# Lent buffers, other PSUM banks and a new step order in a fused chunked-attention and top-1 MoE kernel

## The chip, the cores and the metric

The kernel runs on 1 core of one Trainium2 chip, as one launch. The metric is the device time in microseconds (us) of one execution. Three runs of the kernel before stand beside the one execution that the profiler recorded. PE is TensorE, DVE is VectorE, ACT is ScalarE, POOL is GpSimd, and SP is the engine whose queue issues nearly all loads and stores.

## The reference

Attention inside chunks of 64 rows, then a mixture of 8 experts in which each token takes one expert. A token whose local gate is 0.5 or more takes over the expert of the token before it.

```
q, k, v: (8, 8, 576, 64)                      # batch, heads, rows, head size; fp32
per chunk of 64 rows: attn = softmax(q k^T / 8); x = attn v
x: (8, 576, 512)                              # heads side by side
logits = x w_gate (512 x 8); gate = sigmoid(x w_local)
e[s] = argmax(logits[s])  if s == 0 or gate[s] < 0.5  else  e[s-1]
out[s] = softmax(logits[s])[e[s]] * (relu(x[s] w1[e]) w2[e])     # w1: 512 x 1024, w2: 1024 x 512
```

## The kernel before, in words

**Attention.** The 4608 rows are 18 blocks of 256 rows. Each block loads q, k and v (512 KB each), pairs the heads anew (`pair_heads`, POOL copies into `qr`, `kr`), transposes them on PE (`trans4`, L195, into `qT`, `kT`), forms scores (L230) and the softmax (`pr`), transposes P (L195, into `pT`), multiplies with v (`values`, L279, into `xs`), transposes x (`xT`), forms the router's logits (`router`: L321, a copy to `lT`, the transposes L330, a reduction), and stores x with its logits to `x_d` in DRAM (528 KB, L343). One block in each nine, at place `LEFT`, holds the 64-row remainders of four batches and is loaded in other pieces (L146). v lies in pieces of 64 floats (256 B) in DRAM.

The order of steps is written by hand in `PAR`: "start", then "steady" once per i = 1 to 15 (L869), then "drain". A word such as `tp*8` takes the next eight parts of the step `tp`. In iteration i the words mean: `lq` loads q and k of block i+5 and `lv` loads v of block i+2 (SP); `s` scores of i+1; `va` values of i-1; `tx` transposes of x(i-2); `tq` transposes of q and k of i+2; `ra` the router of i-2 (its first part L321, its second L330 and the store); `tp` transposes of P(i); `pr` POOL's copies of i+3; `h0` to `h3` are places at which routing steps run ("hooks": 4 times the iteration, plus the place). Every engine and SP's queue work in exactly this order. q and k have three buffer pairs, so the load of block i+5 waits for POOL's copies of block i+2; v has three buffers (one of them lies in `raw2`), so the load of v(i+2) waits for the values of block i-1.

**Drain and routing.** The last blocks run through "drain" together with the routing: `ex` is a list of DVE operations whose last results are `regs` (L953, L929), words that every engine reads into registers to decide branches (`word` L983, `test` L990), and `ehot` (L950).

**Experts.** Tokens come by expert in tiles of 128, gathered from `x_d`. Each product has three passes with weights split into a high and a low part. `two(a)` works on two tiles: `up_pair` (L1040, matmuls L1046) if both have the same expert, else `up` for each, then `next_x`, which transposes the x of the next tiles (L688), `h_atoms`, which transposes the hidden layer `hsb` (L688), and `down` (L743), whose scaled output `ysb` (L1074) is scattered to `out` (L804). PSUM has eight banks: `TR[0..2]`, two of `HB`, two `YB`, one `MB`. After the pairs, `rest(t)` takes tile after tile, with a `VALID` test that leaves when no tile is left.

Of the kernel before, what the change touches and what calls it, by code (L numbers as in the profile page):

```python
# [8 lines left out]
F32 = mybir.dt.float32  # L9
# [29 lines left out]
LEFT = 4  # L39
# [12 lines left out]
        "p0*4 t0a*4 t0a t0b*4 t0b t0c*4 t0c t0d*4 t0d p1*4 q3 t1a*4 t1a s0*8 t1b*4 t1b s0*2 t1c*4 t1c "  # L52
        "q4 t1d*4 t1d p2*4 s0*4 s1*8 t2a*4 t2a t2b*4 t2b s1*2 o0*4 o0 o0*4 o0 s1 t2c*4 t2c t2d*4 t2d s1*3 q5 v2 p3*4 io "
# [18 lines left out]
    "steady": "lq va*4 va s*8 s h0 tx*8 tq*8 s h1 va*4 lv ra*2 va h2 tq*8 ra*2 tp*8 s pr*4 h3 ",  # L72
    "hooks": [43, 43, 45, 46, 47, 48, 49, 49, 51, 51, 52, 53, 54, 55, 55, 56, 57, 58, 59, 61, 61, 62],
# [4 lines left out]
def tile_attention_then_moe(ctx: ExitStack, tc, q, k, v, wg, wl, w1, w2, out):  # L78
# [17 lines left out]
    w2h = [wpool.tile([P, 2, C], F32R, name=f"w2h{c}") for c in range(4)]  # L96
    w2l = [wpool.tile([P, 2, C], F32R, name=f"w2l{c}") for c in range(4)]
# [27 lines left out]
    vbuf = [[raw2[c].rearrange("p f (h d) -> p (f h) d", d=2 * D) for c in (2, 3)]]  # L125
# [29 lines left out]

    def load_v(i):
        vt = vbuf[i % 3]
        t0 = 0
        for b, s0, n in place(i)[1]:
            for s1 in range(s0, s0 + n, P):  # L160
                m = min(P, s0 + n - s1)
                nc.sync.dma_start(
                    vt[t0 // P][t0 % P:t0 % P + m, :, 0:D],
                    v[b, :, s1:s1 + m, :].rearrange("h s d -> s h d"),
                )
                t0 += m
        return vt
# [191 lines left out]
    cnt = cpool.tile([P, E], F32, name="cnt")  # L359
# [187 lines left out]
    const = {}  # L547

    def constants():
        pcol = iota([P, 1], [[0, 1]], cm=1, name="pcol")  # L550
        pcol1 = iota([P, 1], [[0, 1]], base=1, cm=1, name="pcol1")
        iota_r = iota([P, P], [[1, P]], dst=pa2.tile([P, P], BF16, name="iota_r", tag="xT", bufs=1))
# [29 lines left out]
        const.update(pcol=pcol, pcol1=pcol1, iota_m=iota_m, iota_h=iota_h, iota_hp=iota_hp, iota_t=iota_t, iota_e=iota_e, idxm8=idxm8, padidx=padidx, upper=upper, ones=ones, zrow=zrow, notfirst=notfirst, hot0=hot0)  # L582
# [10 lines left out]
    nc.sync.dma_start(wg9[:, :, 0:8], wg.rearrange("(c p) e -> p c e", p=P))  # L593
    nc.sync.dma_start(wg9[:, :, 8:9], wl.rearrange("(c p) e -> p c e", p=P))
    with tc.manual_schedule(engines=MAN | {ET.Pool}):
        warm = cpool.tile([P, 1], F32, name="warm")
# [15 lines left out]
        st |= dict(  # L612
            io=lambda: [constants], s0=lambda: a_sa(0, True), q3=load(qk, load_qk, 3),
            s1=lambda: a_sa(1, True), o0=lambda: a_tp(0, True), q4=load(qk, load_qk, 4), q5=load(qk, load_qk, 5),
            v2=load(vts, load_v, 2))
        for i in range(3):
            for g in range(4):
                st[f"t{i}{'abcd'[g]}"] = lambda i=i, g=g: tq(i, g)
        play(PAR["start"], st)
    pcol, pcol1, iota_m, iota_h, iota_hp, iota_t, iota_e, idxm8, padidx, upper, ones, zrow, notfirst, hot0 = (  # L620
        const[n] for n in "pcol pcol1 iota_m iota_h iota_hp iota_t iota_e idxm8 padidx upper ones zrow notfirst hot0".split())
# [247 lines left out]
    for i in range(1, NS - 2):  # L869
# [58 lines left out]
    def plus(o, a, k, b):  # L928
# [21 lines left out]
        lambda: V.tensor_tensor(ehot, te[:, 0:NTILE].unsqueeze(2).to_broadcast([P, NTILE, E]),  # L950
                                iota_e.unsqueeze(1).to_broadcast([P, NTILE, E]), ALU.is_equal),
# [7 lines left out]
        plus(regs[:, 0], flags[:, 3, 0:NTILE], VALID, sums[:, 0]),  # L959
    ]  # L960
# [79 lines left out]
    def up_pair(a, f0):  # L1040
        hbs = [(f, TR[f // 2 % 3]) for f in (f0, f0 + 2)]
# [57 lines left out]
    def two(a):  # L1099
# [17 lines left out]
        def next_x():  # L1117
            atoms = [x_atoms(a + 2 + n, ps) for n, ps in enumerate((TR[1], MB)[:1 + (a + 2 in PAIRS)])]
            for f in atoms:
                run(f[:2])  # L1120
            late_x[:] = [f[2] for f in atoms]

        def second():
            run(pr[:2])
            with tc.If(test(a, SAME, WORK)) as cmp:
                up_pair(a, 4)
                next_x()
            with cmp.Else():
                for g in range(2):
                    run(h_atoms(a, g, TR[1 - g]))  # L1130
                rejoin_h(a)
                up(a + 1)
                next_x()
                for g in range(2):
                    run(h_atoms(a + 1, g, TR[2 - 2 * g]))
# [8 lines left out]
        rejoin_h(a + 1)  # L1144

    def body(t):
# [20 lines left out]
        down(t - 1, (3,), (1,))  # L1167

    def rest(t):
        if t == NTILE:  # L1170
            down(t - 1)
            return
        if t < TMIN:
            body(t)
            rest(t + 1)
            return
        with tc.If(test(t, VALID, ALL, want=0)) as cmp:  # L1177
            nc.gpsimd.drain()
            down(t - 1)
        with cmp.Else():  # L1180
            body(t)
            rest(t + 1)
# [5 lines left out]
    with tc.manual_schedule(engines=MAN | {ET.SP, ET.Pool}):  # L1188
# [29 lines left out]
        rest(PAIRS[-1] + 2)  # L1218
# [21 lines left out]
```

## Time and profile before

| | |
|---|---|
| median of three runs | 644.95 us (644.72 to 646.14) |
| the profiled execution | 645.8 us |
| its span in the trace | 643.8 us, mean granted clock 0.996 |
| PE busy | 608.2 us, 94% of the span |
| DVE, ACT, POOL busy | 380.1 (59%), 256.4 (40%), 146.8 us (23%) |
| DMA packets | 78355, of them 42672 under 512 B |

The span is the time between the first and the last instruction in the trace; the other 2.0 us of the profiled execution lie around it. In a list of instructions "[0.80 <-ACT hsb L789]" says that the engine stood idle for 0.80 us before the row and that the operation of line 789 on ACT, which writes `hsb`, ended the wait. In the table of windows, "16.80 (x401)" is busy time and the number of instructions.

### The profile page before, as it was taken

How to read it: one execution, taken by the hardware profiler on the slowest of the kernel's cores; microseconds unless marked ns; L12 is line 12 of the kernel's file. 1: busy time of each engine (PE TensorE's matmuls, PEld its weight loads, DVE VectorE, ACT ScalarE, POOL GpSimd, SP SyncE). 2: the span in 40 equal slices, each digit the busy share in tenths (PEclk: the TensorE clock that was granted, in tenths of full speed). 3: DMA queues.
4: the chain of work that ended last, by engine and by line, in shares of the span. 5: the costliest groups of instructions: out<-in, count | busy, mean ns of one | idle time of the engine just before them, and what ended most of it. 6: DMA issues, size and time to landing. Idle time of an engine off the chain costs nothing. (4 is left out here: it accounts for less than half of the span.)

```text
span 643.8 us, 17179 instructions
## 1 busy us (share of the span) xinstructions
PE 608.2 (94%) x5904; PEld 513.8 (80%) x5904; DVE 380.1 (59%) x990; ACT 256.4 (40%) x468; POOL 146.8 (23%) x217
## 2 busy tenths in 40 slices
PE   4898898999999999999999999999999999999995
PEld 4787776776778878689899997789988998688883
DVE  2676676996785757476433565773478533387231
ACT  4676685774411152532212433431365211343120
POOL 3632253570060302022021021022011221011201
PEclk9999998999999999999999999999999999999999
DMA  8899999989531155055121164441176511054100
GB/s 261 231 261 291 255 273 303 311 244 305 167 125 43 53 167 181 20 182 179 37 69 52 28 217 152 150 175 49 43 240 225 192 52 59 29 184 145 67 26 35
DMA packets 78355, 97.83 MB, mean 152 GB/s; under 512 B 42672, under 2 KB 46768, under 8 KB 78192
## 3 DMA queue, kind: packets, MB, share of 16 engines
q1 hardware_dynamic: 71744, 75.30, 37.7%
q0 software_dynamic: 6160, 19.99, 9.3%
q8 instruction: 84, 1.38, 0.9%
q14 instruction: 79, 0.65, 0.3%
q10 hardware_dynamic: 288, 0.52, 0.3%
HBM read 76.62 MB, written 19.69 MB: 150 GB/s over the span
## 5 line engine op out<-in xcount | busy, mean ns | idle before, releaser
L804 POOL DMA_INDIRECT out<-ysb,sidx x38 | 40.2, 1058 | 359.6 <-DVEq L1024 160.9
L743 PE MATMUL y<-w2h,hq 128*128 128x512 f32 x368 | 119.8, 395 | 1.8 <-DVE ysb L1074 1.8
L1046 PE MATMUL tr<-xp,w1h 128*128 128x256 f32 x704 | 90.1, 283 | 1.5 <-ACTq L1024 1.5
L1046 PEld LDWEIGHTS tr<-xp,w1h 128*128 128x128 f32 x704 | 87.8, 192 | 4.4 <-ACTq L1024 1.9
L743 PEld LDWEIGHTS y<-w2h,hq 128*128 128x128 f32 x368 | 69.1, 188 | 17.2 <-issue 3.0
L743 PE MATMUL y<-w2l,hq 128*128 128x512 f32 x184 | 71.8, 390 | 0.0
L1054 ACT ACTIVATE hq<-tr 128x256 fp32r<-128x256 f32 x68 | 25.3, 384 | 110.0 <-PE tr L1046 76.5
L743 PE MATMUL y<-w2h,hp 128*128 128x512 f32 x192 | 63.3, 397 | 0.3 <-ACT hp L690 0.3
L722 PE MATMUL h<-w1h,xp 128*128 128x512 f32 x208 | 60.5, 396 | 0.0
L1055 DVE SCALAR_TENSOR_TENSOR hq<-tr,hq 128x256 fp32r<-128x256 f32 x68 | 28.2, 423 | 41.3 <-ACT hq L1054 38.9
L1046 PE MATMUL tr<-xp,w1l 128*128 128x256 f32 x352 | 47.6, 283 | 0.0
L1074 DVE TENSOR_SCALAR ysb<-y,ppr 128x512 f32<-128x512 f32 x33 | 24.8, 750 | 36.0 <-PE y L743 31.7
L1046 PEld LDWEIGHTS tr<-xp,w1l 128*128 128x128 f32 x352 | 44.6, 192 | 0.0
L722 PEld LDWEIGHTS h<-w1h,xp 128*128 128x128 f32 x208 | 38.1, 188 | 7.4
L694 POOL DMA_INDIRECT xg<-x_d,gidx x36 | 38.5, 1070 | 20.2 <-issue 13.5
L743 PEld LDWEIGHTS y<-w2h,hp 128*128 128x128 f32 x192 | 36.0, 188 | 8.1 <-ACT hp L690 0.5
L789 ACT ACTIVATE hsb<-h 128x512 f32<-128x512 f32 x26 | 14.1, 596 | 66.2 <-PE h L722 45.3
L743 PEld LDWEIGHTS y<-w2l,hq 128*128 128x128 f32 x184 | 34.6, 188 | 6.6 <-DVE w2l L1014 0.2
L1014 DVE TENSOR_TENSOR w1l<-raw,w1h 128x1024 fp32r<-128x1024 f32 x28 | 32.4, 1219 | 8.7 <-ACT w1h L1007 6.8
L743 PE MATMUL y<-w2l,hp 128*128 128x512 f32 x96 | 37.5, 390 | 0.0
L1014 DVE TENSOR_TENSOR w2l<-raw,w2h 128x1024 fp32r<-128x1024 f32 x28 | 32.7, 1220 | 1.5 <-issue 1.2
L1007 ACT CAST w2h<-raw 128x1024 fp32r<-128x1024 f32 x28 | 28.3, 1048 | 11.8 <-DMA raw<-in_moe_w 3.9
(224 smaller groups left out, 1059.4 us busy)
## 6 DMA issues: line engine op xcount, KB each, us to landing
raw<-in_moe_w SPq DMA_DIRECT2D x72, 512.0 KB, 5.2
x_d<-xs SPq DMA_DIRECT2D x16, 528.0 KB, 6.3
qt<-in_q SPq DMA_DIRECT2D x32, 256.0 KB, 4.8
kt<-in_k SPq DMA_DIRECT2D x30, 256.0 KB, 4.8
v<-in_v SPq DMA_DIRECT2D x20, 256.0 KB, 5.4
raw<-in_v SPq DMA_DIRECT2D x12, 256.0 KB, 5.2
x_d<-xs SPq DMA_DIRECT2D x4, 264.0 KB, 3.9
qt<-in_q SPq DMA_DIRECT2D x8, 128.0 KB, 3.6
```

The source lines that it names most:

```text
L694: nc.gpsimd.indirect_dma_start(out=dst, out_offset=None, in_=src, in_offset=bass.IndirectOffsetOnAxis(ap=gidx[t].bitcast(U32), axis=0))
L722: nc.tensor.matmul(hs[:, j], xs[a][:, c], W1[w][c][:, 512 * j:512 * j + 512], start=(c == 0 and n == 0), stop=(c == 3 and n == 2))
L743: nc.tensor.matmul(y, h_of(t, f // 4)[a][:, f % 4], W2[w][c][:, f % 2, :], start=(f == 0 and n == 0), stop=(f == 7 and n == 2))
L789: nc.scalar.activation(hsb[:, 512 * j:512 * j + 512], hs[:, j], AF.Relu)
L804: nc.gpsimd.indirect_dma_start(out=out, out_offset=bass.IndirectOffsetOnAxis(ap=sidx[t].bitcast(U32), axis=0), in_=ysb, in_offset=None, bo ...
L1007: nc.scalar.copy(hi[c], raw[c])
L1014: V.tensor_tensor(lo[c], raw[c], hi[c].bitcast(F32), ALU.subtract)
L1046: nc.tensor.matmul(hb[:, 256 * n:256 * n + 256], W1[w][c][:, P * (f + n):P * (f + n) + P], XP[:, x, c].rearrange("p s t -> p (s t)"), star ...
L1054: nc.scalar.activation(hi, ps, AF.Relu)
L1055: V.scalar_tensor_tensor(lo, ps, 0.0, hi.bitcast(F32), ALU.max, ALU.subtract)
L1074: V.tensor_scalar(ysb, y, pr, None, ALU.mult)
```

## The change

- **Buffers.** q and k get six buffer pairs instead of three (the three more, `lent[0:3]`, lie in the memory that w2's split copies take later), v gets four instead of three (`lent[3]` is the new one).
- **Start.** The loads of q, k of blocks 3, 4, 5, v of block 2 and the router's weights stand at the front; POOL's constants move from the start to behind iteration i = 2.
- **Steady order.** v's loads in front of q's and k's; the scores' eight parts in front of the first values; the logits' transposes (second `ra*2`) behind P's (`tp*8`).
- **Places.** `LEFT` is 6 instead of 4, and the two steps of the carry row move from hook 49 to hook 50.
- **Drain.** `ex*8` is taken earlier, and `ehot` becomes the last of that list.
- **Banks.** `up_pair` takes TR0, TR1, HB, TR2 instead of TR0, TR1, TR2, TR0; the second x of `next_x` takes TR0 instead of MB; the hidden layer's transposes take TR2, TR0 and TR2, MB instead of TR1, TR0 and TR2, TR0.
- **End.** In `rest` a tile's output (scale and scatter) stands behind the test for the next tile; when the loop leaves, the last tile's matmuls stand in front of the output of the tile before.

```
-LEFT = 4
+LEFT = 6
 "start": (
-  "p0*4 t0a*4 ... p1*4 q3 t1a*4 ... q4 t1d*4 ... t2d s1*3 q5 v2 p3*4 io "
+  "q3 v2 q4 wg q5 p0*4 t0a*4 ... p1*4 t1a*4 ... t1d*4 ... t2d s1*3 p3*4 "
-  "steady": "lq va*4 va s*8 s h0 tx*8 tq*8 s h1 va*4 lv ra*2 va h2 tq*8 ra*2 tp*8 s pr*4 h3 ",
-  "hooks": [43, 43, 45, 46, 47, 48, 49, 49, 51, 51, ...
+  "steady": "lv lq s*8 va*4 va s h0 tx*8 tq*8 s h1 va*4 ra*2 va h2 tq*8 tp*8 ra*2 s pr*4 h3 ",
+  "hooks": [43, 43, 45, 46, 47, 48, 50, 50, 51, 51, ...
...
+lent = [[wpool.tile([P, 8 * 2 * D], F32, name=f"lent{nm}{c}", tag=f"w2{nm}{c}", bufs=1) for nm in "hl"] for c in range(4)]
+qkbuf = [[pe2.tile([P, 8 * 2 * D], F32, name=f"{nm}{n}", bufs=1) for nm in ("qt", "kt")] for n in range(3)]
+qkbuf += lent[0:3]
...
+vbuf.append([t.rearrange("p (h d) -> p h d", d=2 * D) for t in lent[3]])
+vbuf.append([raw2[c].rearrange("p f (h d) -> p (f h) d", d=2 * D) for c in (2, 3)])
...
+        qt, kt = qkbuf[i % len(qkbuf)]
...
-        vt = vbuf[i % 3]
+        vt = vbuf[i % len(vbuf)]
...
+        if i == 2:
+            pcol, pcol1, iota_m, ... = constants()
...
-        hbs = [(f, TR[f // 2 % 3]) for f in (f0, f0 + 2)]
+        hbs = [(f, (TR[0], TR[1], HB[:, 0], TR[2])[f // 2]) for f in (f0, f0 + 2)]
...
-            atoms = [x_atoms(a + 2 + n, ps) for n, ps in enumerate((TR[1], MB)[:1 + (a + 2 in PAIRS)])]
+            atoms = [x_atoms(a + 2 + n, ps) for n, ps in enumerate((TR[1], TR[0])[:1 + (a + 2 in PAIRS)])]
...
-        down(t - 1, (3,), (1,))
...
+        def leave():
+            nc.gpsimd.drain()
+            down(t - 1, parts=(0,))
+            if t > FIRST:
+                down(t - 2, (3,), (1,))
+            down(t - 1, parts=(1,))
+
+        def stay():
+            if t > FIRST:
+                down(t - 2, (3,), (1,))
+            body(t)
+            rest(t + 1)
```

Where the instructions stand now, at three places. **PE, one iteration of "steady"** (`o` is values, `sc` scores, `lg` logits, `tr` a bank for transposes of `xs`, `qr`, `kr`, `pr`). Before:

```order
L279 MATMUL o<-v_121,pT 64x65 x16
L230 MATMUL sc<-kT,qT 64x64 x32
L195 MATMUL tr<-ident,xs_440 128x128 x8
L195 MATMUL tr<-ident,qr 128x128 x8
L279 MATMUL o<-v_121,pT 64x65 x16
L321 MATMUL lg<-xT,wg_69 32x256 x4
L195 MATMUL tr<-ident,kr 128x128 x8
L330 MATMUL lg<-ident,lT 128x128 x2
L195 MATMUL tr<-ident,pr 128x128 x8
```

The same iteration after the change:

```order
L233 MATMUL sc<-kT,qT 64x64 x32
L282 MATMUL o<-v_126,pT 64x65 x16
L198 MATMUL tr<-ident,xs_428 128x128 x8
L198 MATMUL tr<-ident,qr 128x128 x8
L282 MATMUL o<-v_126,pT 64x65 x16
L324 MATMUL lg<-xT,wg_69 32x256 x4
L198 MATMUL tr<-ident,kr 128x128 x8
L198 MATMUL tr<-ident,pr 128x128 x8
L333 MATMUL lg<-ident,lT 128x128 x2
```

Between P's transposes and the values that use them now stand the logits' transposes and the scores; before, the values followed at once.

**SP's queue in "steady"**, iterations 4 and 5 (`x_d` is the store of x). Before:

```order
L151 DMA qt<-in_q 128x1x512 x2
L151 DMA kt<-in_k 128x1x512 x2
L162 DMA v_120<-in_v 128x8x64 x2
L343 DMA x_d<-xs_443 128x2x528
L151 DMA qt<-in_q 128x1x512 x2
L151 DMA kt<-in_k 128x1x512 x2
L162 DMA v_121<-in_v 128x8x64 x2
```

The same queue after the change:

```order
L165 DMA v_126<-in_v 128x8x64 x2
L154 DMA lenth_82<-in_q 128x1x512 x2
L154 DMA lentl_83<-in_k 128x1x512 x2
L346 DMA x_d<-xs_425 128x2x528
L102 DMA raw_1_87<-in_moe_w 128x1024
L165 DMA v_127<-in_v 128x8x64 x2
L154 DMA qt_120<-in_q 128x1x512 x2
L154 DMA kt_121<-in_k 128x1x512 x2
```

v's two loads moved from behind the four loads of q and k to in front of them; the store keeps its place at the end.

**DVE at the end of the drain** (`regs` are the words for the branches, `hp` and `xp` the low halves of the first expert tiles' operands). Before:

```order
L810 TENSOR_SCALAR ysb<-y,ppr 128x512
L691 TENSOR_TENSOR hp_3017<-tr,hp_3017 128x512
L691 TENSOR_TENSOR hp_3018<-tr,hp_3018 128x512
L691 TENSOR_TENSOR xp<-tr,xp 128x4x128
L950 TENSOR_TENSOR ehot<-te,iota_e 128x368
L711 TENSOR_SCALAR pm<-psm 128x1
L712 RECIPROCAL pm<-pm 128x1
L713 TENSOR_TENSOR ppr<-psm,pm 128x1
L952 TENSOR_TENSOR flags<-te 1x46
L953 TENSOR_SCALAR regs<-te 1x46
L929 SCALAR_TENSOR_TENSOR flags<-flags 1x46 x5
L929 SCALAR_TENSOR_TENSOR regs<-flags 1x46
```

After the change:

```order
L954 TENSOR_TENSOR flags<-te 1x46
L955 TENSOR_SCALAR regs<-te 1x46
L933 SCALAR_TENSOR_TENSOR flags<-flags 1x46 x5
L933 SCALAR_TENSOR_TENSOR regs<-flags 1x46
L810 TENSOR_SCALAR ysb<-y,ppr 128x512
L691 TENSOR_TENSOR hp_2995<-tr,hp_2995 128x512
L691 TENSOR_TENSOR hp_2996<-tr,hp_2996 128x512
L691 TENSOR_TENSOR xp<-tr,xp 128x4x128
L962 TENSOR_TENSOR ehot<-te,iota_e 128x368
```

The registers' words moved from behind the tiles' operands to in front of the output `ysb`.

## Rows read from the trace of the kernel before

**Rows 1.** Busy time by windows: PE, PEld, DVE, ACT, POOL, granted clock, DMA share, GB/s.

```profile
40.00:60.00 20.00, 17.48 (x449) 14.65 (x448) 12.86 (x32) 13.39 (x23) 5.96 (x11) 1.00 0.95 269
...
100.00:120.00 20.00, 18.85 (x426) 15.60 (x419) 16.44 (x47) 12.94 (x24) 7.20 (x10) 0.94 1.03 302
...
200.00:620.00 420.00, 416.26 (x2505) 357.96 (x2504) 232.74 (x549) 139.01 (x262) 69.90 (x66) 1.00 0.34 113
```

**Rows 2.** PE's waits, 19 to 140 us: total us, times, longest us.

```profile
PE o L279 <- ACT pT L185: 3.4, 11, 0.7
PE o L279 <- DMA v<-in_v: 1.9, 1, 1.9
...
PE sc L230 <- ACT pr L249: 0.7, 1, 0.7
```

**Rows 3.** PE's timeline around iterations 9 to 12: start us, busy us, instructions [idle before].

```profile
81.60 0.70 PE L279 MATMUL o<-v,pT 64*64 64x65 f32 x32 [0.26 <-ACT pT L185]
82.11 1.11 PE L230 MATMUL sc<-kT,qT 64*64 64x64 f32 x64
...
88.84 0.70 PE L279 MATMUL o<-raw,pT 64*64 64x65 f32 x32 [0.26 <-ACT pT L185]
...
94.78 1.04 PE L195 MATMUL tr<-ident,pr 128*128 128x128 f32 x8
96.56 0.33 PE L279 MATMUL o<-v,pT 64*64 64x65 f32 x4 [0.74 <-ACT pT L185]
98.81 1.02 PE L279 MATMUL o<-v,pT 64*64 64x65 f32 x26 [1.93 <-DMA v<-in_v]
...
108.24 0.70 PE L279 MATMUL o<-v,pT 64*64 64x65 f32 x32
```

**Rows 4.** The window behind that stall, columns as in the first group.

```profile
100.00:104.00 4.00, 4.00 (x78) 3.62 (x70) 3.35 (x7) 1.39 (x3) 0.00 (x0) 0.72 1.02 297
```

**Rows 5.** SP's timeline of DMA issues, iterations 4 to 10: start us, us.

```profile
42.45 2.39 SPq L343 DMA_DIRECT2D x_d<-xs  x1
...
92.23 1.17 SPq L162 DMA_DIRECT2D v<-in_v  x2
93.50 1.05 SPq L343 DMA_DIRECT2D x_d<-xs  x1
```

**Rows 6.** SP's waits, 40 to 140 us: total us, times, longest us.

```profile
SPq L343 <- DVE rs L292: 8.8, 5, 2.6
SPq L162 <- PE tr L195: 7.9, 12, 1.6
```

**Rows 7.** DVE's and PE's timelines where the pairs begin.

```profile
191.34 0.75 DVE L810 TENSOR_SCALAR ysb<-y,ppr 128x512 f32<-128x512 f32 x1 [1.08 <-PE y L743]
192.88 1.29 DVE L691 TENSOR_TENSOR hp<-tr,hp 128x512 fp32r<-128x512 f32 x2 [0.79 <-ACT hp L690]
...
195.80 0.99 DVE L929 SCALAR_TENSOR_TENSOR flags<-flags 1x46 f32<-1x46 f32 x5
196.83 0.20 DVE L929 SCALAR_TENSOR_TENSOR regs<-flags 1x46 int32<-1x46 f32 x1
...
198.12 4.10 PE L1046 MATMUL tr<-xp,w1h 128*128 128x256 f32 x32 [1.46 <-ACTq L1024]
```

**Rows 8.** PE's waits, 200 to 620 us, and one of them in PE's timeline.

```profile
PE m L688 <- ACT hsb L789: 1.6, 2, 0.8
PE m L688 <- ACT hsb L785: 1.4, 2, 0.7
...
237.74 0.66 PE L688 MATMUL m<-ident,xg 128*128 128x128 f32 x4 [0.80 <-ACT hsb L789]
238.24 1.04 PE L688 MATMUL tr<-ident,hsb 128*128 128x128 f32 x8
```

**Rows 9.** The timeline of the last tiles, DVE and PE.

```profile
631.23 0.75 DVE L1074 TENSOR_SCALAR ysb<-y,ppr 128x512 f32<-128x512 f32 x1 [0.92 <-DVEq L997]
...
632.13 0.47 PE L743 MATMUL y<-w2h,hq 128*128 128x512 f32 x1 [1.77 <-DVE ysb L1074]
```

More of the change, by code (lines that the diff above doesn't have):

```diff
@@ L95, in tile_attention_then_moe @@
     w1l = [wpool.tile([P, F], F32R, name=f"w1l{c}") for c in range(4)]
-    w2h = [wpool.tile([P, 2, C], F32R, name=f"w2h{c}") for c in range(4)]
-    w2l = [wpool.tile([P, 2, C], F32R, name=f"w2l{c}") for c in range(4)]
+    w2h, w2l = [], []
+    lent = [[wpool.tile([P, 8 * 2 * D], F32, name=f"lent{nm}{c}", tag=f"w2{nm}{c}", bufs=1) for nm in "hl"] for c in range(4)]
     raw1 = [wpool.tile([P, F], F32, name=f"raw1_{c}") for c in range(4)]
@@ L123, in tile_attention_then_moe @@
     ps_l = ctx.enter_context(tc.tile_pool(name="ps_l", bufs=1, space=PSUM))
-    vbuf = [[raw2[c].rearrange("p f (h d) -> p (f h) d", d=2 * D) for c in (2, 3)]]
+    qkbuf = [[pe2.tile([P, 8 * 2 * D], F32, name=f"{nm}{n}", bufs=1) for nm in ("qt", "kt")] for n in range(3)]
+    qkbuf += lent[0:3]
+    vbuf = []
     for i in range(2):
@@ L358, in tile_attention_then_moe @@
     rq = pa1.tile([P, 2, NT], F32, name="rq")
-    cnt = cpool.tile([P, E], F32, name="cnt")
+    cnt = cpool.tile([P, 2 * E], F32, name="cnt")[:, 0:E]
     nc.gpsimd.memset(cnt, 0.0)
@@ L545, in iota @@
         return t
-    const = {}
     def constants():
@@ L551, in constants @@
         pcol1 = iota([P, 1], [[0, 1]], base=1, cm=1, name="pcol1")
-        iota_r = iota([P, P], [[1, P]], dst=pa2.tile([P, P], BF16, name="iota_r", tag="xT", bufs=1))
+        iota_r = iota([P, P], [[1, P]], dst=raw1[3][:, 0:P])
         iota_m = iota([P, P], [[0, 2], [1, HT]], dt=BF16, name="iota_m")
@@ L592, in tile_attention_then_moe @@
             vts[i - 1] = load_v(i - 1)
[L593 to L594 removed]
     with tc.manual_schedule(engines=MAN | {ET.Pool}):
[L596 removed]
+        warm = pa2.tile([P, 1], F32, name="warm", tag="xT", bufs=1)
         nc.scalar.activation(warm, ident[:, 0:1], AF.Exp)
@@ L612, in tile_attention_then_moe @@
         st |= dict(
-            io=lambda: [constants], s0=lambda: a_sa(0, True), q3=load(qk, load_qk, 3),
+            s0=lambda: a_sa(0, True), q3=load(qk, load_qk, 3),
             s1=lambda: a_sa(1, True), o0=lambda: a_tp(0, True), q4=load(qk, load_qk, 4), q5=load(qk, load_qk, 5),
@@ L618, in tile_attention_then_moe @@
                 st[f"t{i}{'abcd'[g]}"] = lambda i=i, g=g: tq(i, g)
+        st |= dict(wg=lambda: [lambda: (
+            nc.sync.dma_start(wg9[:, :, 0:8], wg.rearrange("(c p) e -> p c e", p=P)),
+            nc.sync.dma_start(wg9[:, :, 8:9], wl.rearrange("(c p) e -> p c e", p=P)))])
         play(PAR["start"], st)
-    pcol, pcol1, iota_m, iota_h, iota_hp, iota_t, iota_e, idxm8, padidx, upper, ones, zrow, notfirst, hot0 = (
-        const[n] for n in "pcol pcol1 iota_m iota_h iota_hp iota_t iota_e idxm8 padidx upper ones zrow notfirst hot0".split())
     gidx, sidx = {}, {}
@@ L877, in tile_attention_then_moe @@
         play(" ".join(toks), qs4 | {k: v for k, v in opt.items() if v is not None})
+        if i == 2:
+            pcol, pcol1, iota_m, iota_h, iota_hp, iota_t, iota_e, idxm8, padidx, upper, ones, zrow, notfirst, hot0 = constants()
         if i in (4, 6, 8, 10):
@@ L892, in tile_attention_then_moe @@
         load_w2(0, c)
+    for nm, ts in (("h", w2h), ("l", w2l)):
+        ts.extend(wpool.tile([P, 2, C], F32R, name=f"w2{nm}{c}", tag=f"w2{nm}{c}", bufs=1) for c in range(4))
     n = NS - 1
@@ L1129, in second @@
                 for g in range(2):
-                    run(h_atoms(a, g, TR[1 - g]))
+                    run(h_atoms(a, g, TR[2 - 2 * g]))
                 rejoin_h(a)
@@ L1134, in second @@
                 for g in range(2):
-                    run(h_atoms(a + 1, g, TR[2 - 2 * g]))
+                    run(h_atoms(a + 1, g, (TR[2], MB)[g]))
         refill(1, (a, BEFORE), second)
@@ L1166, in body @@
         rejoin_h(t)
-        down(t - 1, (3,), (1,))
     def rest(t):
[L1170 to L1173, printed above, removed]
+        def leave():
[7 more added lines that the diff above has]
+                down(t - 2, (3,), (1,))
             body(t)
             rest(t + 1)
[L1176 to L1182, printed above, removed]
+        if t == NTILE:
+            leave()
+        elif t < TMIN:
+            stay()
+        else:
+            with tc.If(test(t, VALID, ALL, want=0)) as cmp:
+                leave()
+            with cmp.Else():
+                stay()
     mix = {t: (t, MIXED) if t >= EARLY else None for t in range(NTILE)}
@@ L1217, in tile_attention_then_moe @@
                 nc.gpsimd.drain()
-        rest(PAIRS[-1] + 2)
+        rest(FIRST)
 _INS = ["q", "k", "v", "moe_w_gate", "moe_w_local", "moe_w1", "moe_w2"]
```

15 lines of the change are left out of this document (7 added, 8 removed), and 2 rows, old and new, of the table PAR.

## The prediction, made before the changed kernel was run

> **What bounds the kernel now.** I read the busy time by windows first, then PE's waits, then PE's and SP's timelines at the waits that the change names. From 200 to 620 us PE works 416.26 of 420 us [rows 1]: there the experts' matmuls set the pace, and a change gains only what PE still waits. In the attention PE works 17.48 of 20 us in one window, while the 16 DMA engines are 0.95 busy at 269 GB/s [rows 1]. So two things are close to the end there: PE's order, with small waits in each iteration, and the loads. PE's waits from 19 to 140 us are led by the values, which wait 11 times, 3.4 us in all, for ACT's copy of the transposed P, and once 1.9 us for a load of v [rows 2]. The timeline shows an ordinary iteration, from values to values, at 88.84 - 81.60 = 7.24 us, and the one with v's load at 108.24 - 96.56 = 11.68 us [rows 3]. That stall cost more than its 1.93 us: the window behind it has PE busy throughout at a granted clock of 0.72, a mix of the levels 2.4 and 1.2 GHz [rows 4]. SP, which issues the loads, is itself held up: v's loads waited 7.9 us for PE to free a v buffer, and the stores of x 8.8 us for one DVE line [rows 6]. SP's order explains the stall: v(10) was issued at 92.23 us, behind all the loads of q and k, and PE wanted it at 96.56 [rows 3, 5].
>
> **The change, part by part.** All sums are made against the profiled execution, 645.8 us; it lies 0.85 us above the median of the three runs, 644.95.
>
> *Steady order and buffers (attention).* PE issues the same transposes, scores and values, in another order; SP moves the same bytes.
> (1) Between P's transposes and the values now stand the logits' transposes and the scores, 1.11 us of work [rows 3]. The waits for ACT's copy are 0.26 to 0.74 us [rows 2, 3], so they are covered: at most 3.4 us gained. If the scores are themselves late, for lack of kT, the cover is gone and nothing is gained.
> (2) v's two loads go in front of q's and k's four and find a free buffer, so the stall for v should go: at most 11.68 - 7.24 = 4.4 us with its slow clock [rows 3]. The routing steps that run in that iteration are paid one place later and are not counted as gain.
> (3) In iteration 1 the scores waited 0.70 us for ACT [rows 2]. They now come before the first half of the values, whose step is 82.11 - 81.60 = 0.51 us [rows 3]: the wait grows by 0.5 us.
> For PE alone that is 3.4 + 4.4 - 0.5 = 7.3 us. The loads bound it from the other side. From the store of block 0 at 42.45 us to that of block 6 at 93.50, six blocks took 51.05 us [rows 5], 8.5 us each, although PE's own period is 7.24. A block is 3 x 512 KB of loads and 528 KB of store; with two weight loads of 512 KB the six make 13.7 MB, or 269 GB/s, the same as in the window table. If the DMA engines can do no more, the attention ends when it ended before: gain 0. At the 302 GB/s of the best window [rows 1] the six blocks would take 13.7 MB / 302 GB/s = 45.5 us: gain 5.6. Which it is hangs on why SP waited. The waits for PE, 7.9 us, go with the fourth v buffer; the waits for DVE, 8.8 us [rows 6], stay, since x's store keeps its place behind the loads. About half of what held the queue is removed, so I take half of 5.6, **3.0 us**, and keep 0 and 7.3 as ends. What is late next is q and k of the blocks after the eighth or so: PE will have run ahead of them, and POOL's copies should then wait for their loads.
> (4) The constants that move behind iteration 2 lie on POOL, an engine that is busy 5.96 of 20 us there [rows 1]; that cover would have to vanish for them to cost. The earlier wg load, the two more memsets, `LEFT`, the other place of the carry row and the padded `cnt` move no work onto PE, and I cost them at nothing.
>
> *Drain.* PE's first pair of tiles waits 1.46 us until ACT has read the registers [rows 7]. The instructions that write them took 0.99 + 0.20 = 1.2 us on DVE and stood in front of the last low half of x; they now stand ahead of `ysb`, where DVE had idled 1.08 and 0.79 us [rows 7], so they delay nothing. Gain **1.2 us**, between 0 (x's low half or ACT's read sets the start anyway) and 1.46.
>
> *Banks.* In four pairs the second x waited for the relu, 1.6 + 1.4 us in all [rows 8], since its bank MB is one that a form of the relu reads (L785); TR0 was emptied long before. The transposes into it, 238.24 - 237.74 = 0.50 us [rows 8], then run inside that wait; the transposes of `hsb` still wait for the relu, which writes it. So 4 x 0.5 = **2.0 us**, between 0 and 3.0. New behind it: the next `up_pair` begins in TR0, and must wait until ACT and DVE have copied the second x out. A whole `down` of matmuls stands between, which covers it; without that cover each pair would begin late.
>
> *End.* The last tile's matmuls waited 1.77 us, until DVE had scaled the tile before; DVE began that only at 631.23, itself behind its branch [rows 9]. With the matmuls in front, PE starts about when DVE left the branch, 632.13 - 631.23 = 0.90 us earlier, or at best 1.77. I take **1.2**, nearer to 0.90, since a branch and POOL's drain still stand ahead; 0 is the lower end.
>
> *Sum:* 3.0 + 1.2 + 2.0 + 1.2 = 7.4 us. 645.8 - 7.4 = 638.4 for the profiled execution, and 0.85 less for the median: **637.5 us**. The extremes of the terms add up to 0 and 7.3 + 1.46 + 3.0 + 1.77 = 13.5, or 645.0 and 631.4.
>
> **The rivals.** Times are medians.
>
> *The loads give back everything.* The DMA engines are 0.95 to 1.03 busy [rows 1]; more buffers let a load begin sooner but move no byte less. Then the attention ends as before, and only 1.2 + 2.0 + 1.2 = 4.4 us remain: 644.95 - 4.4 = 640.5. Against it: the same mix of pieces ran at 302 GB/s from 100 to 120 us. The Trainium skill ("DMA: Bandwidth & Descriptors", section Specifications) says that transfers below 512 B do not reach the full rate, and v comes in pieces of 256 B in both kernels; by that rule the order of the loads changes nothing and the time is this rival's. The trace bears it out only in part: with the same pieces the rate was 269 in one window and 302 in another [rows 1].
>
> *PE's order is all that counts.* If SP's freed waits suffice for the loads, the whole 7.3 us come: 7.3 + 4.4 = 11.7, or 633.3. For it: the stall for v is one of order and not of rate. Against it: 8.5 us per block against 7.24.
>
> *The boundaries do not do what they say.* Each of the three waits outside the attention could be replaced at once by another (x's low half, the relu, the branch). Then 3.0 us remain: 642.0.
>
> *Slower: q and k come too late.* With v in front, q and k of each block are issued later by v's two issues, 1.17 us [rows 5], and PE runs ahead of them in the first iterations. Once the lead is used up, POOL's copies wait for their load, PE stalls with no work to put between, and its clock falls as it did behind v's stall. Such a stall cost 4.4 us [rows 3, 4]. The rest of the change gives 7.3 + 4.4 = 11.7 then, so three stalls, 13.2 us, decide: 644.95 + 1.5 = 646.5, and more with a fourth. For it: the queue is near its limit. Against it: three more buffer pairs let these loads start without POOL's leave, and a wait that is spread over iterations leaves the clock alone (iterations with waits of 0.26 us show it).
>
> **How the numbers follow.** Chances: my forecast 0.45, loads give back everything 0.20, PE's order alone 0.15, boundaries give nothing 0.10, slower 0.10. The range runs from 632.0 (below the full gain's 633.3) to 643.5 (above the 642.0 of the fourth case, by the spread of the runs); it leaves out the slower case and the outer ends of the others, together 0.2. The bound for faster and slower, 0.2%, is 1.3 us, about what a measurement of this kernel can tell from no change: 643.7 and 646.2. Faster takes the first three cases and 0.03 of the fourth, 0.83; the same takes the rest of the fourth and 0.01 of the slower case, 0.08; slower 0.09.
>
> **What would show it.** Right: no waits of the values for ACT's pT, nor for v's load; periods near 7.0 us in the first iterations and of 7.5 to 9 us around iterations 8 to 13, with POOL waiting for DMA there; the first pair's wait down from 1.46 to about 0.3 us; in the four pairs a wait of 0.3 us in front of the transposes of `hsb` instead of 0.7 to 0.8 in front of x's; the last matmuls not released by `ysb`. The end of the last "steady" iteration, about 3 us earlier, decides between the first three cases. Wrong: windows with a granted clock below 0.9 after iteration 7, DMA shares that fall while PE waits, waits of `up_pair` for a copy of x, or a POOL that holds PE when the constants run.

## The result, and the profile after

The changed kernel takes 651.41 us (median of 19 runs, 645.97 to 656.4), the kernel before 644.72 us in the same comparison (19 runs, 642.34 to 647.66): a ratio of 1.0109, 95% interval 1.0091 to 1.0126. It is slower by 1.1%, outside the predicted range. The profiled execution took 652.83 us with a span of 651.0, against 645.8 and 643.8.

The span is cut at three places that both traces have: the scores of the last block (they end the steady part), the first pair of expert tiles, and the last low half of the hidden layer.

| part of the span | before, us | after, us | change | predicted |
|---|---|---|---|---|
| start to the scores of block 17 | 139.44 | 146.77 | +7.33 | -3.0 |
| from there to the first pair | 58.68 | 57.69 | -0.99 | -1.2 |
| from there to the last low half | 431.50 | 430.23 | -1.27 | -2.0 |
| from there to the end | 14.18 | 16.31 | +2.13 | -1.2 |
| sum | 643.8 | 651.0 | +7.2 | -7.4 |

These are single executions. In the profile of e8 below, whose attention is that of the kernel before, the scores of block 17 come at 134.78 us, so the first row is good to some us only; the medians differ by 6.7 us.

The busy time by windows after the change (PE, PEld, DVE, ACT, POOL, granted clock, DMA share, GB/s):

```profile
20.00:40.00 20.00, 17.84 (x478) 15.24 (x480) 14.35 (x33) 14.13 (x25) 9.83 (x39) 1.00 0.80 217
40.00:60.00 20.00, 20.00 (x475) 16.67 (x472) 14.29 (x38) 14.41 (x26) 7.32 (x20) 1.00 0.95 269
...
100.00:120.00 20.00, 16.46 (x385) 12.76 (x382) 14.16 (x43) 12.62 (x23) 8.76 (x12) 1.00 0.92 252
120.00:140.00 20.00, 14.09 (x316) 11.15 (x308) 15.66 (x51) 11.55 (x21) 11.94 (x19) 1.00 0.88 252
...
200.00:620.00 420.00, 417.98 (x2516) 358.64 (x2515) 234.61 (x560) 139.66 (x265) 70.80 (x66) 1.00 0.35 116
```

The last window of the attention in the kernel before, the one behind that of 302 GB/s [rows 1]:

```profile
120.00:140.00 20.00, 19.10 (x456) 15.60 (x458) 18.93 (x71) 14.76 (x26) 14.77 (x21) 1.00 0.95 266
```

From 40 to 60 us PE has no idle time at all; the windows of the second half are the loss: where the kernel before moved 302 and 266 GB/s, this one moves 252 twice, and PE is busy 16.46 and 14.09 of 20 us. The 302 is the best window of that profile; the mean of the five windows from 40 to 140 us is 278 GB/s before and 266 after. PE's timeline after the change, three steady scores, the first stall and the scores of block 17:

```profile
49.73 1.16 PE L233 MATMUL sc<-kT,qT 64*64 64x64 f32 x64
...
56.76 1.16 PE L233 MATMUL sc<-kT,qT 64*64 64x64 f32 x64
...
63.90 1.16 PE L233 MATMUL sc<-kT,qT 64*64 64x64 f32 x64
...
93.01 0.69 PE L282 MATMUL o<-v,pT 64*64 64x65 f32 x32 [2.35 <-DVE xs L296]
...
146.77 0.81 PE L233 MATMUL sc<-kT,qT 64*64 64x64 f32 x40
```

The period is 7.03 us, as forecast, and no values wait for pT or for v's load any more [rows 2]. At 93 us they wait instead for DVE's `xs`, the scaled values; this is PE's largest wait between 20 and 150 us (total us, times, longest us):

```profile
PE o L282 <- DVE xs L296: 5.6, 5, 2.4
```

DVE's timeline and its waits, 40 to 150 us, tell why:

```profile
92.27 0.69 DVE L296 TENSOR_TENSOR xs<-o,rs 128x512 f32<-128x512 f32 x1 [3.17 <-DMA x_d<-xs]
...
DVE xs L296 <- DMA x_d<-xs: 12.3, 7, 3.9
```

The same row of the kernel before, DVE's waits in the same stretch:

```profile
DVE xs L293 <- DMA x_d<-xs: 0.3, 1, 0.3
```

x has four buffers, and DVE may write block i's x only when the store of block i-4 has landed. These stores are late. SP's timeline after the change, around 90 us (start us, us):

```profile
86.43 0.54 SPq L346 DMA_DIRECT2D x_d<-xs  x1
87.07 0.41 SPq L165 DMA_DIRECT2D lenth<-in_v  x1
87.57 0.99 SPq L165 DMA_DIRECT2D lentl<-in_v  x1
88.66 3.88 SPq L154 DMA_DIRECT2D qt<-in_q  x2
92.63 1.20 SPq L154 DMA_DIRECT2D kt<-in_k  x2
93.92 1.31 SPq L350 DMA_DIRECT2D x_d<-xs  x2
```

DVE's wait at 92.27 us ends with the landing of the first of these, the store of block 5. SP issued it at 83.53 us in the kernel before and at 86.43 here, although PE had run some 4 us ahead by then (scores of block 9 at 70.93 us against 74.87). The next store, of block 6, comes at 93.92 us, no earlier than before [rows 5]. SP now stands at q's loads, 3.88 us for two issues that take 1.2 when nothing holds them.

At the end of the span the change also lost. The timeline of DVE and POOL there:

```profile
641.23 1.41 DVE L1078 TENSOR_SCALAR ysb<-y,ppr 128x512 f32<-128x512 f32 x2 [5.85 <-PE y L743]
642.26 0.98 POOL L804 DMA_INDIRECT out<-ysb,sidx  x1 [16.10 <-DMA out<-ysb,sidx]
646.27 0.97 POOL L804 DMA_INDIRECT out<-ysb,sidx  x1 [3.03 <-POOLq L1193]
```

PE did not wait [rows 9], but the output of the tile before now stands behind the last matmuls on DVE as well, so that two scatters follow each other at the end, the second 3.03 us behind the first's end. What held the second for so long the profile does not show. Before, the last scatter began 0.27 us after its `ysb`, at 638.95.

The first pair's wait of 1.46 us and the four of 0.7 to 0.8 us [rows 7, 8] are gone; PE's waits from 200 us on:

```profile
204.46 3.99 PE L1050 MATMUL tr<-xp,w1h 128*128 128x256 f32 x32
...
PE tr L688 <- DVEq L1001: 0.9, 1, 0.9
PE y L743 <- DVE hq L1059: 0.3, 1, 0.3
```

### The profile page after: what moved, and what is told of

Read it like the earlier page. It is cut to its first block, busy times and chain, and to the rows that moved or that the text cites. A ratio compares the mean times of both kernels' runs of the same rounds, so it can differ in the third digit from the quotient of the medians.

```text
span 651.0 us, 17189 instructions
## 1 busy us (share of the span) xinstructions
PE 611.3 (94%) x5904; PEld 514.6 (79%) x5904; DVE 380.2 (58%) x990; ACT 255.7 (39%) x468; POOL 146.8 (23%) x219
## 5 line engine op out<-in xcount | busy, mean ns | idle before, releaser
L1050 PE MATMUL tr<-xp,w1h 128*128 128x256 f32 x528 | 67.0, 283 | 0.0
L1050 PEld LDWEIGHTS tr<-xp,w1h 128*128 128x128 f32 x528 | 65.5, 192 | 1.2 <-ACT w2h L1011 0.4
L1058 ACT ACTIVATE hq<-tr 128x256 fp32r<-128x256 f32 x51 | 18.9, 384 | 68.4 <-PE tr L1050 44.8
L1059 DVE SCALAR_TENSOR_TENSOR hq<-tr,hq 128x256 fp32r<-128x256 f32 x51 | 21.1, 423 | 32.3 <-ACT hq L1058 28.2
L691 DVE TENSOR_TENSOR xp<-tr,xp 128x512 fp32r<-128x512 f32 x39 | 25.5, 686 | 18.6 <-ACT xp L690 15.8
L1050 PE MATMUL tr<-xp,w1l 128*128 128x256 f32 x264 | 35.3, 283 | 0.0
L1050 PEld LDWEIGHTS tr<-xp,w1l 128*128 128x128 f32 x264 | 33.3, 192 | 0.0
```

What stands on the lines that cost most here:

```text
L691: lambda: V.tensor_tensor(lo, box["ps"], hi.bitcast(F32), ALU.subtract)]
L1050: nc.tensor.matmul(hb[:, 256 * n:256 * n + 256], W1[w][c][:, P * (f + n):P * (f + n) + P], XP[:, x, c].rearrange("p s t -> p (s t)"), star ...
L1058: nc.scalar.activation(hi, ps, AF.Relu)
L1059: V.scalar_tensor_tensor(lo, ps, 0.0, hi.bitcast(F32), ALU.max, ALU.subtract)
```

## The experiments

Ratios are to the kernel before, run beside it on the same chip. "Waits" are DVE's waits for stores of x; the first pair's start stands for the end of attention and drain (198.12 us before, 204.46 in the changed kernel).

| run | median us | ratio (95% interval) | waits us | first pair us |
|---|---|---|---|---|
| e1 store in front of q, k | 645.43 | 1.0029 (1.0007 to 1.0051) | none | 196.58 |
| e2 fifth xs buffer | 672.3 | 1.0441 (1.0408 to 1.0474) | none | - |
| e3 no lent buffers | 658.25 | 1.0235 (1.0197 to 1.0273) | none | - |
| e4 old end | 652.18 | 1.0130 (1.0082 to 1.0178) | 9.5 | 203.00 |
| e5 fifth xs buffer, again | 658.43 | 1.0212 (1.0178 to 1.0246) | none | 206.36 |
| e6 three pairs | 652.43 | 1.0088 (1.0056 to 1.0121) | 17.5 | 207.25 |
| e7 LEFT 4 | 653.48 | 1.0124 (1.0097 to 1.0150) | 11.1 | 203.07 |
| e8 before, banks and drain alone | 641.53 | 0.9956 (0.9933 to 0.9979) | 0.8 | 194.52 |
| e9 v at its old place | 641.94 | 0.9968 (0.9941 to 0.9995) | 1.0 | 194.83 |
| e10 old PE order | 649.30 | 1.0072 (1.0039 to 1.0104) | 10.9 | 203.63 |
| e11 fifth xs buffer, third | 647.98 | 1.0061 (1.0035 to 1.0088) | 4.1 | 200.59 |
| e12 e1 and old end | 643.18 | 0.9997 (0.9968 to 1.0026) | none | 196.89 |
| e13 split store, v first | 651.63 | 1.0132 (1.0097 to 1.0167) | 13.2 | 204.36 |
| e14 split store, v last | 644.44 | 1.0034 (1.0014 to 1.0054) | 0.6 | 193.45 |
| e15 e9 and old end | 639.88 | 0.9957 (0.9935 to 0.9980) | 1.2 | 196.58 |

**Are the late stores the cause?** e1 moves q's and k's loads behind the store:

```
-    "steady": "lv lq s*8 va*4 va s ... tp*8 ra*2 s pr*4 h3 ",
+    "steady": "lv s*8 va*4 va s ... tp*8 ra*2 lq s pr*4 h3 ",
```

> In the changed kernel, DVE waits 12.3 us in seven places (40 to 150 us) for stores of x to free an xs buffer; before it was 0.3 us. This run moves the loads of q and k of each iteration behind the store of x in SP's queue, nothing else. Theory A (queue place: the stores stand behind loads that run ahead): these waits fall below 3 us, the scores of the last steady iteration come at 140 us or earlier (146.8 in the changed kernel, 139.4 before), and the time falls to 641 to 646. Theory B (rate: the DMA engines cannot do more, whatever comes first): q and k are late instead, POOL waits for them, and the time stays within 2 us of the changed kernel's 651.4. Theory C (PE order: values and logits' transposes come later, so x does): the waits stay near 12 us and the time within 2 us.

The waits vanish and the attention is 8 us shorter, at 645.43 us. But against the kernel before nothing is won. What came instead are the q and k of theory B. POOL's waits for their loads are no longer than in the changed kernel (its two largest, 40 to 150 us, are 20.3 us there and 19.0 here, 12.2 there and 12.4 here), but now they reach PE: its matmuls wait for POOL, which in the changed kernel they do not. POOL's waits, 40 to 150 us, and PE's, 20 to 150 us:

```profile
POOL qr L190 <- DMA lenth<-in_q: 19.0, 4, 5.6
POOL qr L190 <- DMA qt<-in_q: 12.4, 3, 4.7
...
PE tr L198 <- POOL qr L190: 3.8, 3, 2.3
PE tr L198 <- POOL kr L190: 2.0, 2, 1.0
```

The second test gives x a fifth buffer. It was made three times. e2 is e5 with block 5's load in front of block 0's copies, so that block 0 is computed from block 5's data and starts 21 us late; its time says nothing of the question.

```
-NX = 4
+NX = 5
-    ... for nm in ("qt", "kt")] for n in range(3)]
+    ... for nm in ("qt", "kt")] for n in range(2)]
-            rows.extend(pa2.tile([P, XS], ...) for n in range(NX))
+            rows.extend((pa2 if n < 4 else pe2).tile([P, XS], ...) for n in range(NX))
-        xss[i] = rows[i % NX]
+        xss[i] = rows[i % NX if i < 14 else i - 14]                              # e2, e5
+        xss[i] = rows[(2, 3, 0, 1, 4)[i % 5] if i < 10 else i % 4]               # e11
-        "q3 v2 q4 wg q5 p0*4 t0a*4 ...
+        "q3 v2 q4 wg p0*4 q5 t0a*4 ...                                           # e5, e11
```

> The changed kernel with a fifth xs buffer for blocks 4 to 13 (two pairs of q and k buffers of its own instead of three make the room, so five pairs in all). Theory A (late stores hold xs): DVE's waits for stores fall from 12.3 us to below 4 and the time to 644 to 647. Theory B (rate): the wait goes to another load (POOL for q and k, PE for v) and the time stays at 649 or more. Theory C (PE order): as theory A, since a later x is taken up by a fifth buffer too.

> The fifth xs buffer once more. In the run before, five buffer pairs with the start's order of the changed kernel let block 5's load take block 0's buffer ahead of its copies, so the first copies waited 28.7 us for the loads; here the load of block 5 stands behind block 0's copies in the program, with SP's order as in the changed kernel. Theory A (late stores hold xs): DVE's waits for stores fall from 12.3 us to below 3 and the scores of the last steady iteration come at 140 us or earlier, time 643 to 647. Theory B (rate): PE runs ahead until q, k or v are late, the end of the steady part stays above 143 us, time 648 or more.

> The fifth xs buffer with other numbers: in the run before, the last steady scores came at 139.1 us, but then the hidden layer of the first expert tile, which takes over the memory of one xs buffer, waited 7.0 us for the store of block 16, which that run's numbering had put there. Here block 14 lies there, as in the changed kernel. Theory A: no waits of DVE for stores, last steady scores at 140 us or earlier, no 7 us wait in the drain, time 643 to 647, as with the store in front. If the time stays above 649, the 7.3 us lost in the attention are not the xs buffers'.

In e5 the waits were gone and the scores of block 17 began at 139.06 us; but its numbering put block 16's x into the memory that the first hidden layer takes over, and PE waited for that (PE's timeline of e5):

```profile
171.86 1.12 PE L688 MATMUL tr<-ident,hsb 128*128 128x128 f32 x4 [6.96 <-ACT hsb L789]
```

e11 mends this: 647.98, with one wait of 4.1 us left. It recovers about half, not all: with most of the stores' waits out of the way, q and k hold PE (6.7 us of waits for POOL). So the stores are where the loss shows first, and relieving them alone does not give it all back; the queue as a whole seems slower, which the next runs test.

**Which part of the change makes the queue slow?** Four parts were taken back alone: the lent q and k buffers (e3, e6), `LEFT` with its hooks (e7), PE's order (e10) and the place of v's loads (e9). In e3 the start still loads blocks 3 to 5 ahead, now into the buffers of blocks 0 to 2 before these are copied, so these three blocks are computed from other data and start late; e6 puts the loads behind the copies.

```
-    qkbuf += lent[0:3]                                                           # e3, e6
-LEFT = 6                                                                         # e7, and hooks 50, 50
+LEFT = 4                                                                         #     back to 49, 49
-    "steady": "lv lq s*8 va*4 va s h0 tx*8 tq*8 s h1 va*4 ra*2 va h2 tq*8 tp*8 ra*2 s pr*4 h3 ",
+    "steady": "lv lq va*4 va s*8 s h0 tx*8 tq*8 s h1 va*4 ra*2 va h2 tq*8 ra*2 tp*8 s pr*4 h3 ",   # e10
+    "steady": "lq s*8 va*4 va s h0 tx*8 tq*8 s h1 va*4 lv ra*2 va h2 tq*8 tp*8 ra*2 s pr*4 h3 ",   # e9
```

> The changed kernel with its three own pairs of q and k buffers alone, the lent ones left out. Theory A: the loads of q and k wait again for POOL's copies, so they run less far ahead, but the store stands behind them in the queue all the same; DVE's waits for stores stay at 6 us or more and the time at 647 to 655. Theory B: the same bytes at the same rate, within 2 us of 651.4. A third case, that the lent buffers are what lets the loads crowd out the stores: waits below 3 us and the time at 645 or less.

> The changed kernel without the lent q and k buffers, three pairs as before, with the loads of blocks 3, 4 and 5 in the program behind the copies that free their buffers; SP's order is the changed kernel's. If the lent buffers are what lets loads run ahead of the stores: DVE's waits for stores below 4 us and time 645 or less. If the stores are late because of their place in the queue alone: waits of 6 us or more, time 649 to 656, since SP now also waits for POOL's copies with the store behind it.

> The changed kernel with LEFT 4 and the carry row's steps at hook 49, as before. The mixed block's eight small loads of 128 KB are issued at about 0.61 us each, so that the DMA engines get at most some 210 GB/s then; in the changed kernel they fall at 29 to 38 us and 107 to 114 us, when the stores wait behind them. Theory D (place of the mixed block): the waits of DVE for stores fall below 8 us and the time by 2 us or more, to 649 or less. Theory A alone: within 2 us of 651.4.

> The changed kernel with PE's old order in the steady part (values before scores, logits' transposes before P's), the loads still v, then q and k. Theory C (x is finished later in each iteration): the waits for stores fall below 5 us and the time to 645 to 648, less than that theory's full gain because the 11 waits for ACT's pT, 3.4 us, come back. Theory A (queue place and rate): PE is slowed by the pT waits, the stores' waits shrink by about as much, 8 to 12 us remain, and the time is within 2 us of 651.4.

> The changed kernel with v's loads back at their old place, behind q's and k's, in SP's queue (PE's new order, the lent buffers, the fourth v buffer and the start stay). Theory E (v in front is what makes the stores late): DVE's waits for stores fall from 12.3 us below 4, the scores of the last steady iteration come at 141 us or earlier, time 643 to 647. Rival (any order that puts the store last): waits of 8 us or more, time 649 to 654.

Only e9 answers: 641.94 us, faster than before, with one word of the order moved. e6 and e7 stay within 2.1 us of 651.4, and e10, at 649.30 with 10.9 us of waits, near it. DVE's waits and the windows of e9:

```profile
DVE xs L296 <- DMA x_d<-xs: 1.0, 3, 0.3
...
100.00:120.00 20.00, 17.32 (x380) 13.53 (x382) 16.01 (x51) 13.82 (x24) 9.20 (x14) 1.00 0.99 288
120.00:140.00 20.00, 16.78 (x428) 13.56 (x422) 19.11 (x66) 13.14 (x24) 12.48 (x18) 1.00 0.95 262
```

288 and 262 GB/s stand where the changed kernel had 252 and 252. The mean of the five windows from 40 to 140 us parts the profiled executions by their order (e2 and e3, which start late, left out). With v first it is 248 to 274 GB/s in eight of them: the changed kernel, e4 to e7, e10, e11, e13. With v behind k, or q and k behind the store, it is 276 to 289 in seven: the kernel before, e1, e8, e9, e12, e14, e15. A PE that stalls also frees buffers later and so lowers the rate; the transfers alone, further down, part the two. e1 and e9 have something in common: written as a circle, v x q k and q k v x are the same order of transfers, and v q k x is another.

**Why does the place of v slow the queue?** The DMAs on SP's queue take eight completion semaphores in turn (the traces of the streams below show it), so each is issued only when the one eight places before has landed, and a block has seven. In the changed kernel that puts q behind the v of the block before; with the store in two DMAs a block has eight, and each waits for its own like.

```
-                nc.sync.dma_start(xv[b, s0:s0 + n].rearrange("(c p) n -> p c n", p=P), xs)
+                for c in range(2):
+                    nc.sync.dma_start(xv[b, s0 + P * c:s0 + P * c + P], xs[:, c])
```

> The changed kernel (v's loads first) with each store of x as two DMAs of 264 KB. SP keeps at most eight DMAs under way: each waits for the one eight places before it. With seven per block in the order v v q q k k x, the first q waits for the v of the block before; with eight per block, each waits for its own like. Theory F (which DMA waits for the slow v pieces): the rate comes back, DVE's waits for stores fall below 5 us, the time to 643 to 647. Theory G (the order of the transfers in itself, or the larger lead of the loads over the store): the waits stay at 8 us or more and the time at 649 to 653.

> The control: v's loads at their old place, as in the run that gave 641.9, with each store as two DMAs. If splitting itself costs or gains (two issues, smaller pieces in flight), it shows here: same within 1.5 us of 641.9 by theories F and G both; 644 or more if eight smaller DMAs under way carry less.

With v first the loss stays (651.63), and with v last the split itself costs a little (1.0034 against 0.9968). The pairing is not it. The traces of the streams that follow agree: there every issue began 1.5 us or more after the DMA eight places before had landed, so this wait held nothing.

Then the transfers were run alone, three kernels that differ in one string; they load and store 16 blocks and compute nothing:

```
+ORDER = "vqkx"        # e16; "qkvx" in e17, "qvkx" in e18
...
+    for i in range(16):
+        for c in ORDER:
+            step[c](i)
```

> The transfers alone: 16 blocks of q, k, v loads and x stores (2.1 MB each, 33.8 MB), in the changed kernel's order v q k x, on SP's queue, nothing computed and out left unwritten but for 256 rows. Theory G1 (the order of the transfers in itself lowers the rate): this stream takes at least 5 us longer than the one in the order q k v x. Theory G2 (the order costs only by when the store is issued against the computing): both streams take the same time within 2 us, near 33.8 MB / 285 GB/s = 119 us plus start and end.

> The same transfers in the order q k v x, as in the kernel before. G1: shorter than the other stream by 5 us or more. G2: the same within 2 us; then the DMA engines would have carried the changed kernel's transfers as fast, and what was lost was lost by waiting.

> The transfers alone in a third order, q v k x: v neither right behind a store nor right in front of one. v q k x took 125.7 us, q k v x 113.4. If v's small pieces are slow when they are issued right behind a store, this is near 113 (below 117); if the store has to follow v at once to fill its time, near 126 (above 122); between them, both neighbours count.

v q k x takes 125.72 us (125.24 to 126.88), q k v x 113.35 (110.86 to 114.06), q v k x 119.49 (118.76 to 120.59). SP's timeline in v q k x, one block (start us, us), and v's row of its DMA issues (count, KB each, median us to landing):

```profile
50.24 2.10 SPq L106 DMA_DIRECT2D v<-in_v  x2
52.38 3.54 SPq L99 DMA_DIRECT2D qt<-in_q  x2
55.97 1.25 SPq L99 DMA_DIRECT2D kt<-in_k  x2
57.26 0.59 SPq L110 DMA_DIRECT2D x_d<-xs  x1
57.90 2.23 SPq L106 DMA_DIRECT2D v<-in_v  x2
...
v<-in_v SPq DMA_DIRECT2D x32, 256.0 KB, 6.2
```

The same of q k v x:

```profile
54.45 1.48 SPq L99 DMA_DIRECT2D qt<-in_q  x2
55.98 1.27 SPq L99 DMA_DIRECT2D kt<-in_k  x2
57.29 1.22 SPq L106 DMA_DIRECT2D v<-in_v  x2
58.55 2.78 SPq L110 DMA_DIRECT2D x_d<-xs  x1
61.37 1.39 SPq L99 DMA_DIRECT2D qt<-in_q  x2
...
v<-in_v SPq DMA_DIRECT2D x32, 256.0 KB, 5.2
```

And of q v k x:

```profile
50.11 1.56 SPq L106 DMA_DIRECT2D v<-in_v  x2
51.71 3.01 SPq L99 DMA_DIRECT2D kt<-in_k  x2
```

The order alone is worth 12.4 us in 16 blocks, 0.77 us per block, with the same bytes and pieces and nothing computed to wait for. Between these two orders v lands in 6.2 us instead of 5.2 when it follows the store; the medians of q, k and x differ by 0.2 us at most. The middle order, in which v neither follows nor precedes the store at once, lies half way, so by the reading set down before that run neither neighbour alone decides.

One thing is the same in all three: SP is held longest at whatever stands right behind v's two loads. That is q in v q k x (3.54 us for two issues, where k's take 1.25), the store in q k v x (2.78 us, where it takes 0.59 in the first order) and k in q v k x (3.01 us). This fits the kernels: in the changed one SP stands 3.88 us at q's loads and then issues the store in 0.54, in the one before the hold falls on the store (2.39 us at 42.45 [rows 5]). Why the hold costs more in one place than in another, and why v lands later behind a store, stays open.

**The rest of the change.** e8 puts banks and drain alone into the kernel before; e4, e12 and e15 take the old end back, in the changed kernel, in e1 and in e9.

```
+        hbs = [(f, (TR[0], TR[1], HB[:, 0], TR[2])[f // 2]) for f in (f0, f0 + 2)]   # e8, with the other
+        "... ex*8 h2*2 y1 ...                                                        # banks and ehot last
...
+        down(t - 1, (3,), (1,))                     # e4, e12, e15: at the end of body, as before
-            down(t - 1, parts=(0,))                 # and down(t - 1) alone behind the test
```

> The kernel before with the new banks and the earlier registers alone (attention and end as before). From the changed kernel's trace: from the end of the steady part to the first pair 57.7 us against 58.7 before, and from there to the last low half of the hidden layer 430.2 against 431.5, so 1.0 + 1.3 = 2.3 us faster than before, 0.36%. Rival: as the prediction had it, 1.2 + 2.0 = 3.2 us, 0.50%. Third: no change, the waits come back elsewhere.

> The changed kernel with the old end of the tiles behind the pairs (output at the end of body, the last tile's matmuls behind the output of the tile before). From the last low half of the hidden layer to the end of the span the changed kernel takes 651.0 - 634.7 = 16.3 us, the kernel before 643.8 - 629.6 = 14.2. If the new end is the cause (two scatters that now follow each other only at the very end), this becomes 14.2 again and the time falls by 2.1 us, to 649.3. If it is not, it stays at 16.

> The changed kernel with both remedies: q's and k's loads behind the store, and the old end of the single tiles. The store's place gave 645.4 (ratio 1.003 to before). If the new end costs the 2.1 us that the profiles show, this is 643 to 644, ratio 0.998 to 1.001. If not, it stays at 645 to 646.

> The best of both: the changed kernel with v's loads at their old place and the old end of the single tiles. From 641.9, the end's price in the profiles (2.1 us, or nothing where PE's wait there also slows its clock) gives 640 to 642, ratio 0.993 to 0.997 to before; if the old end gives nothing back, 642.

e8 is faster by 0.44%, 2.8 us. The end is less clear in the times. Against e1, e12 has a ratio lower by 0.0032, 2.1 us, and against e9, e15 one lower by 0.0011; in both pairs the intervals overlap, and e4 shows no gain. The profiles are clearer, and give a reason for the spread. From the last low half to the end of the span, the nine traces of the changed kernel, e1, e6, e7, e9, e10, e11, e13 and e14, which have the new end, take 16.0 to 17.0 us. With the old end it is 14.05 to 14.39 us in three (the kernel before, e8, e15) and 15.56 and 15.68 in e12 and e4. With the old end PE waits for `ysb`, and what follows depends on its clock; a window behind that wait in e12 and the one in e15 (columns as above):

```profile
632.00:634.00 2.00, 2.00 (x6) 1.59 (x5) 0.00 (x0) 0.00 (x0) 0.00 (x0) 0.50 0.09 31
```

```profile
632.00:634.00 2.00, 2.00 (x11) 1.65 (x10) 0.00 (x0) 0.00 (x0) 0.00 (x0) 1.00 0.03 8
```

In e12 PE idled 1.90 us and its granted clock then fell to 0.50, the level of 1.2 GHz; in e15 it idled 1.99 us and the clock stayed at 1.00. e4 went as e12 (1.98 us of idle, then a window at 0.55), the kernel before and e8 as e15 (1.77 us). So the new end trades a stall that sometimes costs clock against a second scatter at the end. e15, at 639.88 us (0.9957), is the best of the runs with e8, and no better than e8: with banks, drain and old end in both, all that the change does to the attention with v in its old place gains nothing that can be told from noise.

## Why the prediction was wrong

- **Steady order and buffers, the steps (1) to (3).** They held as far as PE goes: no value waits for pT or for v, and the period is 7.03 us. (3) also came, a wait of 1.3 us for ACT's `pr` where it had been 0.7.
- **The bound by the loads: the step that failed.** "If the DMA engines can do no more, the attention ends when it ended before: gain 0." That took the rate as a property of the bytes and the pieces. It is one of their order too: moving v's two loads in front lowered it, from a mean of 278 GB/s between 40 and 140 us to 266, and the streams alone show 12.4 us in 16 blocks for the order. The lower end of the term should have been a loss, and no run shows the 5.6 us that were halved, worked out from the best window's 302 GB/s, as a gain of the attention. The words "SP moves the same bytes" were used as if an order could cost nothing, and the steady part came out at +7.33 us in the profile where -3.0 was forecast. The sign "DMA shares that fall while PE waits" came: 0.92 and 0.88 from 100 to 140 us, where it had been 1.03 and 0.95.
- **What is late next.** I named q and k. They were late (POOL's waits for their loads, 0 from 40 us on before, are 41 us in the changed kernel), but PE's matmuls had cover for that and show no wait for POOL there; what reached them was the store of x, the last of each block in the queue, which frees the buffer that DVE writes (5.6 us of PE's waits for `xs`). I had noted that the store keeps its place behind the loads, and gave the waits of 8.8 us no price for the case that PE runs ahead of it.
- **The rivals.** "Loads give back everything" is what e15 shows for the attention, with v back in its place, against e8. The slower rival had the right result, by another mechanism: no q or k stall of 4.4 us with a slow clock, but seven waits for stores. It priced v's place at the 1.17 us of v's two issues; the two issues of q behind them took 3.88 us in the place shown, where 1.2 is usual. The Trainium skill ("DMA: Bandwidth & Descriptors", section Specifications) gives 512 B as the smallest transfer that reaches the full rate. Read as the prediction read it, that makes v's pieces of 256 B cost the same in any order. The streams alone show 125.7 and 113.4 us for the same pieces in two orders: here the order counts too, and the measurement decides. In the chances one step does not hold: the fourth case, 642.0, lies below the bound of 643.7 for faster, but only 0.03 of its 0.10 was counted as faster.
- **Drain.** Right: -0.99 us against -1.2, the wait of 1.46 us gone. **Banks.** Right in kind, the gain smaller than forecast: -1.27 against -2.0 in the profile; e8 has both together at 2.8 us, against 3.2.
- **End.** "0 is the lower end" failed. The sum looked at PE's wait alone. DVE's scaling of the tile before now also stood behind the last matmuls, and its scatter with it, and this made +2.13 us in the profile; the times of e4, e12 and e15 put it at 0 to 2 us.

## What to carry to other kernels

Where a DMA queue is near its limit, the order of its transfers can be part of its rate, as here: time the stream alone in both orders before moving one load in front of another. Ask of every queue which entry comes last in a round and what buffer it frees, above all a store, for an engine that gets faster may run into that one first. A move that takes a wait away from one engine has to be followed on every engine that shares the moved instructions, to the last store of the kernel.

## What the runs showed of the hardware that was not expected

The same 34 MB in the same pieces, on one queue with nothing computed, took 113.4, 119.5 or 125.7 us by the order of four transfers. In each order SP's queue was held, by 3.5, 2.8 or 3.0 us in the blocks shown, at the transfer right behind the loads in 256 B pieces. And an idle time of PE of 1.90 or 1.98 us was followed by a granted clock of 0.50 or 0.55 (e12, e4), but one of 1.99 us by 1.00 (e15).
